# One start of a Fourier filter and ELU kernel, two ways of bringing in the filter

## The chip, the cores and the metric

The kernel runs on one core of a Trainium2 chip. A core has engines with in-order instruction streams of their own: TensorE (PE in the profile, its weight loads PEld), VectorE (DVE), ScalarE (ACT), GpSimd (POOL) and SyncE (SP). SP, ACT and POOL also issue DMA transfers, which all run on the same 16 DMA engines of the core; a transfer that SP issues stands in the queue q1 of the profile, one of ACT's in q10, one of POOL's in q0. Engines wait for one another, and for transfers, on semaphores.

The metric is the device time of one execution in microseconds (us). Before the change it was 2668.45 us, the median of three runs from 2663.02 to 2669.16.

## The reference

Two blocks follow each other. The first filters along the sequence in the frequency domain, the second is a two-layer network with ELU between:

```python
# x: (8, 3008, 256); filt_r, filt_i: (1505, 256)
X = np.fft.rfft(x, axis=1)
Y = X * (filt_r + 1j * filt_i)[None]
y = np.fft.irfft(Y, n=3008, axis=1).astype(np.float32)
# w_in: (256, 2048), w_out: (2048, 256), both float64
h = y.reshape(24064, 256) @ w_in
g = np.where(h > 0, h, np.exp(np.minimum(h, 0)) - 1)
out = (g @ w_out).astype(np.float32)
```

## The kernel before

**The transform.** 3008 is 47 x 64, and the Fourier transform of a batch is done as two small ones by matmul. Step a goes over the 64: six chunks of x, each of up to 2 x 4 values of the 47 (rows i and 47 - i, for the real symmetry), meet a table (ta, tf). Step b goes over the 47 for eight groups g of four frequencies (b_unit): two matmul results, re and im, are multiplied on VectorE by the filter's two parts (L321 to L324). Step bi (bi_unit) goes back over the 47, its result is written to DRAM (y_write, yd) and read back in another order (y_read), and n_unit goes back over the 64. Between a and b there is a turn of the data as well: through DRAM (z) for batches 1 to 7, but by PE transposes (t_first) for batch 0.

**The network.** Each of the six n_units of a batch gives 256 (or 224) columns in each of two halves. Both products use seven multiplications of blocks in place of eight; the sums of weight blocks are made once, in w_join, and the sums of data in combine (L395 to L398) and in the tails of up_steps and down_steps. From the first n_unit on, a list of items (b, m, q) is walked, and the transform of the next batch is placed in between by a plan of quads (`at(quad, place, fn, ...)`). The order within each engine is thus the program's order.

**The start.** Before the first n_unit three things must happen at once. Batch 0 must go through the transform. The weights, 16 groups of 512 KB of float64 (w_fetch, k = 0 to 15), must be brought in and turned into float32 by integer and float operations: w_split on VectorE (L588, L589), w_float on ScalarE (L594 to L599), w_join on VectorE (L605 to L625). Group k is w_in or w_out of quarter q = k // 4. And the filter must lie in the layout of step b: partitions 0 to 47 and 64 to 111, with a row of the spectrum and the mirrored row beside each other.

For batch 0 the filter is read straight from filt_r and filt_i into one large tile ff of all eight groups, by f_read_first: 11 transfers each, filt_r on SP's queue and filt_i on POOL's, with rows of 2 KB and 1 KB. For batches 1 to 7 the filter is first rearranged from DRAM to DRAM into fd (f_arrange, placed at quad 3), and each group is then read from fd by two transfers with rows of 4 KB (f_read) into one of three buffers (fbufs).

The queues in the start: SP has the first half of each x chunk (L236), the table tf (L238), the small tables gr, gi, gf, eye, then filt_r, gb, tn. POOL has the second half of each x chunk (L237), all weight groups and filt_i. A fetch of a weight group waits for its buffer: groups 6 to 11 take the buffers of x chunks 0 to 5 and wait for TensorE's matmuls on them. TICKS says which weight group is turned into float32 at which group g of the b loop; split k and tick(k) (float of k, join of k - 1) stand around the work of group g.

**The end.** The last o_unit transposes on VectorE (L540) and issues 16 stores of 32 KB; for the very last one they go around the queues of SP, ACT and POOL.

The lines that the prediction's steps name are these: L237 x half 1, L300 filter pieces, L321 first product, L341 and L342 evacuations of bi_unit, L350 y_write, L359 y_read, L396 the first combination behind both evacuations of n_unit, L540 and L550 the last transposes and stores, L789 in the profile for the memsets of fbufs.

Of the kernel before, what the change touches and what calls it, by code (L numbers as in the profile page):

```python
# [28 lines left out]
B = 8  # L29
# [12 lines left out]
def _make_tables():  # L42

    n2, k2 = np.arange(N2), np.arange(K2)
    ta, tn = np.zeros((P, H, P)), np.zeros((P, H, P))
    for i in range(H):
        for h in range(2):
            if h and i == 0:
                continue  # L60
            n1 = N1 - i if h else i
            th = 2 * np.pi * (((N1 * n2[:, None] + n1) * k2[None]) % N) / N
            c, s = np.cos(th), -np.sin(th)
            c[:, 0], s[:, 0] = 1.0, 1.0 - 2.0 * (n2 % 2)
# [24 lines left out]
    gb[64:88, 1, 24:48], gb[88:112, 1, 0:24] = -s3, -s0  # L89

    m0, m3 = np.full((24, 1), 2 / N), np.full((24, 1), 2 / N)
    m0[0] = m3[23] = 1 / N
    s0[:, 0] = s3[:, 23] = 0.0
    gr[0:24, 1, 0:24], gr[24:48, 1, 24:48] = m0 * c0.T, m3 * c3.T
    gi[0:24, 1, 24:48], gi[24:48, 1, 0:24] = -m0 * s0.T, -m3 * s3.T
    lie = np.concatenate([2 * np.arange(24), 2 * np.arange(24) + 1])
    gb[:, :, lie] = gb[:, :, :48].copy()
    for t in (gr, gi):
        for o in (0, 64):
            t[o + lie] = t[o:o + 48].copy()  # L100
    gf = np.zeros_like(gb)
    for o in (0, 64):
        gf[o:o + 48] = gb[o:o + 48].reshape(2, H, 2, 64).swapaxes(0, 1).reshape(48, 2, 64)
    return [t.astype(np.float32) for t in (ta, tn, gb, gr, gi, tf, np.eye(P), gf)]


def order(m):
# [5 lines left out]
def kernel(  # L113
# [8 lines left out]
):  # L122
    nc = tc.nc

    ta_d, tn_d, gb_d, gr_d, gi_d, tf_d, eye_d, gf_d = [
        nc.inline_tensor(t, name=n + "_t").ap()
        for t, n in zip(_make_tables(), ("ta", "tn", "gb", "gr", "gi", "tf", "eye", "gf"))
    ]

    def pool(name, bufs, **kw):  # L130
# [17 lines left out]
    psO = pool("psO", 1, space=PSUM)  # L148
    psM = pool("psM", 1, space=PSUM)

    gb, gr, gi = (glob.tile([P, 2, 64], FP32, name=n) for n in ("gb", "gr", "gi"))

    w_in, w_out = ([glob.tile([P, 7, 2, P], FP32, name="%s%d" % (n, i)) for i in range(4)] for n in ("wi", "wo"))

# [63 lines left out]
    def x_place_first(c):  # L218
        if c < XBUFS:
            t = xp.tile([P, 2, 2, D], FP32, tag="xc", name="xc").rearrange("p k u d -> p (k u) d")  # L220
        else:
            t = t1p.tile([P, XC, D], FP32, tag="t1", name="x1")
        if c < 2:
            w = tnp.tile([P, 4, P], FP32, tag="tn", name="tn")
        else:
            if c % 2 == 0:
                tas["pair"] = t4p.tile([P, 4, D], FP32, tag="t4", name="t0").rearrange("p u (w f) -> p (u w) f", f=P)
            w = tas["pair"][:, 4 * (c % 2):4 * (c % 2) + 4, :]
        xs[0, c], tas[0, c] = t, w
        if c == 0:  # L230
            nc.vector.memset(t[HALVES[1], 0, :], 0.0)

    def x_load_first(c):
        t = xs[0, c]
        u = 1 if c == 0 else 0
        nc.sync.dma_start(t[HALVES[0]].rearrange("p u d -> p (u d)"), raw(x, XC * c, [[N1 * D, 64], [1, XC * D]]))  # L236
        nc.gpsimd.dma_start(t[HALVES[1], u:XC, :], raw(x, N1 - XC * c - u, [[N1 * D, 64], [-D, XC - u], [1, D]]))  # L237
        nc.sync.dma_start(tas[0, c], tf_d[:, 4 * c:4 * c + 4, :])  # L238

    def a_first(c):  # L240
        xt, w = xs.pop((0, c)), tas.pop((0, c))
# [39 lines left out]
            k = p * K2 + 4 * g  # L281
            nc.sync.dma_start(t[r:r + 24].rearrange("i u d -> i (u d)"), zs[b][:, k:k + 4, :].rearrange("i u d -> i (u d)"))

    def f_read(b, g):
        t = fbufs[(b * NG + g) % FBUFS]
        for a, r in enumerate((LO, HI)):
            nc.gpsimd.dma_start(t[r].rearrange("p c u d -> p (c u d)"), fd[g, a].rearrange("q c u d -> q (c u d)"))

    def f_read_first(t, c):


        src, queue = ((filt_r, nc.sync), (filt_i, nc.gpsimd))[c]
        for a in ((0, 1), (1, 0))[c]:
            r = a * 64
            queue.dma_start(t[r:r + 48:2, :, c, :, :].rearrange("q g u d -> q g (u d)"),
                            raw(src, 2 * a, [[64 * D, 24], [4 * D, NG], [1, 2 * D]]))
            for u in range(2):
                g0 = 1 if a == u == 0 else 0
                for j, n in ((0, 16), (16, 7)):
                    queue.dma_start(t[r + 1 + 2 * j:r + 2 * (j + n):2, g0:NG, c, u, :],  # L300
                                    raw(src, 64 * (j + 1) - 4 * g0 - 2 * a - u,
                                        [[64 * D, n], [-4 * D, NG - g0], [1, D]]))
            if a == 0:
                queue.dma_start(t[1:48:2, 0, c, 0, :], raw(src, 32, [[64 * D, 24], [1, D]]))

    def tile_mm(ps, table, k, rhs, special):
        for u, w, v in ((0, 1, 1), (1, 1, 0)) if special else ((0, 2, 0),):
# [227 lines left out]
    def o_unit(b, m):  # L535
# [5 lines left out]
                                in_=c.rearrange("p e (j k s) -> p j k e s", k=2, s=32)[:, 0:n, k])  # L541

        o = o.rearrange("p (u f k) e s -> p u f k (e s)", u=4, f=2)
        queues = itertools.cycle((nc.sync, nc.scalar, nc.gpsimd) if (b, m) == (B - 1, 5) else (nc.sync,))
        for k in range(2):
            for u, w, i in ((0, 3, 1), (3, 1, 0)) if m == 0 else ((0, 4, 4 * m),):
                for f in range(1 if i == 0 else 2):
# [7 lines left out]

    wds = {}

    def w_fetch(k):
        q, j = divmod(k, 4)

        if k in (3, 4):
# [11 lines left out]
            srcs = [moe_w_out.bitcast(U32)[ts(4 * q + 2 * (j - 2) + i, P), :] for i in range(2)]  # L573
        for i, s in enumerate(srcs):
            n = 512 // len(srcs)
            nc.gpsimd.dma_start(wd[:, ts(i, n), :].rearrange("p a w -> p (a w)"), s)

# [49 lines left out]
    def f_arrange():  # L627

        for c, src in enumerate((filt_r, filt_i)):
            for a in range(2):  # L630
                nc.gpsimd.dma_start(fd[:, a, 0:48:2, c, :, :].rearrange("g q u d -> q g (u d)"),
                                    raw(src, 2 * a, [[64 * D, 24], [4 * D, NG], [1, 2 * D]]))
                for u in range(2):
                    g0 = 1 if a == u == 0 else 0
                    nc.gpsimd.dma_start(fd[g0:NG, a, 1:47:2, c, u, :].rearrange("g q d -> q g d"),
                                        raw(src, 64 - 4 * g0 - 2 * a - u,
                                            [[64 * D, 23], [-4 * D, NG - g0], [1, D]]))

                g0 = 0 if a else 1
                nc.gpsimd.dma_start(fd[g0:NG, a, 47, c, :, :].rearrange("g u d -> g (u d)"),  # L640
# [4 lines left out]
    with tc.manual_schedule():  # L645


        TICKS = {0: 7, 1: 8, 2: 9, 3: 10, 4: 11, 5: 12, 7: 13, 8: 14, 9: 15}
        with tc.tile_pool(name="boot", bufs=1) as bp:
            ff = bp.tile([P, NG, 2, 2, D], FP32, name="ff")  # L650
            eye = bp.tile([P, P], FP32, name="eye")
            gf = bp.tile([P, 2, 64], FP32, name="gf")
            pq = [bp.tile([P, 2, D], FP32, name="pq%d" % i) for i in range(2)]
            zt[0] += [bp.tile([P, 16 * ROWS], FP32, name="zt%d" % i) for i in range(2)]

            for z in zt[0] + zt[1]:
                nc.gpsimd.memset(z.rearrange("p (k r) -> p k r", r=ROWS)[:, :, 48:64], 0.0)
            for c in range(NXC):
                x_place_first(c)
            for c in range(NXC):  # L660
                x_load_first(c)
                if c < 5:
                    w_fetch(c)
            nc.scalar.memzero(ff[:, 0:NG // 2])
            nc.vector.memset(ff[:, NG // 2:NG], 0.0)
            wtmp.append([kp.tile([P, 512], U32, tag=t, name=n) for t, n in (("k0", "wm"), ("k1", "we"))] +
# [3 lines left out]
                        [t1p.tile([P, XC, D], FP32, tag="t1", name="wfl").rearrange("p (a b) d -> p a (b d)", a=2)])  # L670
            for i, v in enumerate((1151.0 * 2 ** 23, 255.0 * 2 ** 23)):
                nc.vector.memset(edges[:, i:i + 1], v)
            for t, d in ((gr, gr_d), (gi, gi_d), (gf, gf_d), (eye, eye_d)):
                nc.sync.dma_start(t, d)
            f_read_first(ff, 0)

            def tick(k):
                w_float(k)
# [2 lines left out]
            for c in range(NXC):  # L681
# [2 lines left out]
                a_first(c)  # L684
                if c > 0:
                    w_join(c - 1)
                    w_fetch(c + 4)
                if c == 2:
                    f_read_first(ff, 1)
            for k in range(NXC + 4, 14):  # L690
                w_fetch(k)
            for g in range(4):
                t_first(g)
            w_split(NXC)
            tick(NXC)
            w_fetch(14)
            nc.sync.dma_start(gb, gb_d)
            tn_read(0, 0)
            for g in range(NG + 2):
                k = TICKS.get(g)  # L700
# [11 lines left out]
                    y_read(0, 0, (nc.sync, nc.scalar))  # L712
                if k:
                    tick(k)
                if g == 0:
                    w_fetch(15)
        w_join(15)
        for c in range(2):
            x_load(1, c)
# [13 lines left out]

        for c in range(2, XBUFS):
            at(c - 2, 0, x_load, 1, c)
        at(3, 1, f_arrange)
        for f in fbufs:
            at(4, 1, nc.vector.memset, f, 0.0)
        for b in range(B):
# [82 lines left out]
```

## Time and profile before

| | us |
|---|---|
| median of three runs | 2668.45 |
| profiled execution, own time | 2667.55 |
| its span | 2665.7 |
| PE busy | 2598.2 (97%) |
| DVE busy | 1843.5 (69%) |
| ACT busy | 1507.6 (57%) |
| POOL busy | 250.5 (9%) |

All times within the profile count from the begin of the span. Busy times of PE are those of pipelined matmuls with modelled ends. The share of the DMA engines is a mean over 16. "Issue" as a cause of idle time means that the profile shows nothing that the engine waited for. A group of instructions is named by the line that issues it, the engine, the operation, and the tiles, written ones first.

### The profile page before, as it was taken

Reading aid. Unit: us, or ns where it says so; the run is one execution under the profiler, and the core shown is the slowest. Engines: PE = TensorE matmul, PEld = TensorE weight load, DVE = VectorE, ACT = ScalarE, POOL = GpSimd, SP = SyncE. Lnnn points to the kernel's source line nnn. Section 1 sums busy time; section 2 is a strip of 40 time slices with the busy share of each in tenths; the row PEclk is TensorE's granted clock in tenths of the full one; section 3 lists DMA queues with packets and bytes.
Section 4 is the critical chain, followed back from the end, with each engine's and each line's share of the span. In section 5 each row is a group of like instructions: output and inputs, shape, how many; then the busy total and the mean of one; then the engine's idle time right before and its main releaser. Section 6 shows DMA issues by size and latency. Waiting matters only on the chain.

```text
span 2665.7 us, 37329 instructions
## 1 busy us (share of the span) xinstructions
PE 2598.2 (97%) x13508; PEld 2211.9 (83%) x13508; DVE 1843.5 (69%) x3203; ACT 1507.6 (57%) x2622; POOL 250.5 (9%) x305
## 2 busy tenths in 40 slices
PE   4799999999999999999999999999999999999998
PEld 3488789888898878988889878898789887898887
DVE  4876767677676776667766676676767677666665
ACT  5655555555555555555555555555555555555554
POOL 3031200012000120002100021001210011000000
PEclk7799999999999999999999999999999999999999
DMA  9454311443124221333314232133321233110010
GB/s 244 114 132 113 100 44 38 102 104 86 38 58 123 76 81 40 95 86 83 77 39 102 73 101 71 38 87 101 99 55 38 75 82 85 39 40 19 22 27 16
DMA packets 229272, 202.87 MB, mean 76 GB/s; under 512 B 132312, under 2 KB 195467, under 8 KB 229089
## 3 DMA queue, kind: packets, MB, share of 16 engines
q1 hardware_dynamic: 210449, 163.00, 24.6%
q0 software_dynamic: 17616, 36.87, 5.5%
q8 instruction: 107, 1.75, 0.3%
q10 hardware_dynamic: 1024, 0.62, 0.1%
q14 instruction: 76, 0.62, 0.1%
HBM read 128.45 MB, written 74.97 MB: 76 GB/s over the span
## 4 chain that ended last, share of the span: by engine, by line
PE 95%; DMA 2%; DVE 2%; ACT 0%; issue 0%; POOL 0%; POOLq 0%; SPq 0%; DVEq 0%; ACTq 0%
PE po L502 43%; PE phs L420 25%; PE phd L420 12%; PE pha L420 6%; PE psn L372 3%; PE pva L309 2%; PE psr L309 2%; PE psa L207 2%; DMA wd<-in_moe_w_out_dram 0%; DMA ff<-in_filt_i_dram 0%; DMA f<-in_moe_w_in_dram 0%; DMA wd<-in_moe_w_in_dram 0%; DMA f<-in_moe_w_out_dram 0%; PE pvb L309 0%; PE psi L309 0%
## 5 line engine op out<-in xcount | busy, mean ns | idle before, releaser
L502 PE MATMUL po<-g,wo 128*128 128x256 f32 (+1 forms) x5376 | 1296.7, 375 | 0.0
L502 PEld LDWEIGHTS po<-g,wo 128*128 128x128 f32 x5376 | 1015.0, 190 | 129.5 <-issue 16.2
L431 ACT ACTIVATE g<-phs 128x512 f32<-128x512 f32 (+1 forms) x576 | 338.7, 588 | 843.8 <-PE phs L420 843.1
L428 DVE TENSOR_TENSOR g<-phd,g 128x512 f32<-128x512 f32 (+1 forms) x384 | 259.6, 676 | 463.9 <-ACT e L438 278.1
L438 ACT ACTIVATE e<-e 128x512 f32<-128x512 f32 (+1 forms) x768 | 477.3, 621 | 24.3
L420 PE MATMUL phs<-y,wi 128*128 128x256 f32 (+1 forms) x1536 | 395.4, 380 | 0.0
L420 PE MATMUL phs<-ys,wi 128*128 128x256 f32 (+1 forms) x1536 | 387.7, 375 | 1.5 <-ACT g L431 1.5
L442 DVE SCALAR_TENSOR_TENSOR g<-e,g 128x512 f32<-128x512 f32 (+1 forms) x576 | 387.1, 672 | 0.2 <-ACT e L438 0.2
L437 ACT ACTIVATE e<-g 128x512 f32<-128x512 f32 (+1 forms) x576 | 352.8, 613 | 35.3 <-DVE g L428 29.2
L420 PEld LDWEIGHTS phs<-y,wi 128*128 128x128 f32 x1536 | 285.1, 190 | 83.2 <-ACT t L341 34.1
L420 PEld LDWEIGHTS phs<-ys,wi 128*128 128x128 f32 x1536 | 291.4, 190 | 35.4 <-ACT g L431 2.5
L442 DVE SCALAR_TENSOR_TENSOR g<-e,phs 128x512 f32<-128x512 f32 (+1 forms) x192 | 129.9, 676 | 139.1 <-ACT e L438 139.1
L420 PE MATMUL phd<-ys,wi 128*128 128x256 f32 (+1 forms) x768 | 193.9, 375 | 1.8 <-DVE g L428 1.8
L420 PE MATMUL phd<-y,wi 128*128 128x256 f32 (+1 forms) x768 | 193.7, 375 | 0.0
L420 PE MATMUL pha<-y,wi 128*128 128x256 f32 (+1 forms) x768 | 193.7, 375 | 0.0
L437 ACT ACTIVATE e<-phs 128x512 f32<-128x512 f32 (+1 forms) x192 | 112.9, 588 | 141.9 <-PE phs L420 141.0
L330 POOL TENSOR_TENSOR sr<-sr,sp 128x512 f32<-128x512 f32 x56 | 71.2, 1271 | 1243.3 <-DVE sp L323 1243.3
L420 PEld LDWEIGHTS phd<-ys,wi 128*128 128x128 f32 x768 | 145.7, 190 | 18.9 <-DVE g L428 2.5
L420 PEld LDWEIGHTS pha<-y,wi 128*128 128x128 f32 x768 | 145.9, 190 | 16.6
L420 PEld LDWEIGHTS phd<-y,wi 128*128 128x128 f32 x768 | 145.8, 190 | 16.5
L479 DVE TENSOR_TENSOR g<-g,g 128x512 f32<-128x512 f32 (+1 forms) x192 | 130.8, 681 | 6.7
L482 DVE TENSOR_TENSOR g<-g,g 128x512 f32<-128x512 f32 (+1 forms) x192 | 130.6, 680 | 6.6
(143 smaller groups left out, 2403.4 us busy)
## 6 DMA issues: line engine op xcount, KB each, us to landing
yd<-t SPq DMA_DIRECT2D x127, 192.0 KB
t<-yd SPq DMA_DIRECT2D x190, 128.0 KB
z<-t SPq DMA_DIRECT2D x84, 256.0 KB
f<-fd POOLq DMA_DIRECT2D x112, 192.0 KB, 3.6
t<-z SPq DMA_DIRECT2D x224, 96.0 KB
out_dram<-o SPq DMA_DIRECT2D x630, 32.0 KB
tn<-tn_t SPq DMA_DIRECT2D x48, 256.0 KB
xc<-in_x_dram SPq DMA_DIRECT2D x84, 128.0 KB
```

Source lines behind the costliest of these rows:

```text
L309: nc.tensor.matmul(ps[:, u:u + w, :], table[k, v, :], r[k, u:u + w, :], start=n == 0, stop=n == len(rhs) - 1)
L330: nc.gpsimd.tensor_tensor(out=sr, in0=sr, in1=p, op=ALU.add)
L372: nc.tensor.matmul(ps[:, ts(q, P)], t[:, i - 4 * m, ds(dh * P, P)], w[:, i - 4 * m, :], start=True, stop=True)
L420: nc.tensor.matmul(ps[:, a, 0:h], w_in[q][:, COMBO[n], a, :], y[n], start=start and a == 0, stop=True, skip_group_check=True)
L428: nc.vector.tensor_tensor(out=g[o], in0=i0, in1=i1, op=ALU.add)
L431: nc.scalar.activation(out=g[o], in_=i0, func=AXT.Copy)
L437: nc.scalar.activation(out=e, in_=src, func=AXT.Relu, scale=-1.0)
L438: nc.scalar.activation(out=e, in_=e, func=AXT.Exp, scale=-1.0)
L442: nc.vector.scalar_tensor_tensor(out=g[n], in0=es[n], scalar=1.0, in1=src, op0=ALU.subtract, op1=ALU.max)
L479: nc.vector.tensor_tensor(out=b12, in0=b22, in1=b12, op=ALU.subtract)
L482: nc.vector.tensor_tensor(out=g["t4"], in0=g["b21"], in1=g["t2"], op=ALU.subtract)
L502: nc.tensor.matmul(po[i][:, u, 0:h], w_out[q][:, COMBO[n], a, :], g[n][:, a, :], start=q == 0 and a == 0 and n in (1, 3, 6, 4), stop=True, ...
```

## The change

The filter is rearranged by f_arrange first of all, on POOL's queue ahead of every other transfer, and batch 0 reads its groups from fd by f_read into the eight parts of ff. f_read_first is gone. In f_arrange the pieces of 23 rows are split in 16 and 7, so that it has 28 transfers in place of 20. Weight groups 0 to 7, both halves of x and all tables go by SP's queue; POOL has, behind the rearrangement, groups 8 and 9, and then groups 10 to 13 in between the reads of the filter. The tables gb, gr, gi are one transfer (gs), eye and gf another (once), and the table tf comes in double chunks from chunk 2 on. Weight groups 6 and 7 are split and converted before the b loop rather than in it, and TICKS shifts: three of the groups now come after the last product. The 16 last stores go by SP and ACT.

```diff
@@ x_load_first(c)
-        nc.gpsimd.dma_start(t[HALVES[1], u:XC, :], raw(x, N1 - XC * c - u, [[N1 * D, 64], [-D, XC - u], [1, D]]))
-        nc.sync.dma_start(tas[0, c], tf_d[:, 4 * c:4 * c + 4, :])
+        nc.sync.dma_start(t[HALVES[1], u:XC, :], raw(x, N1 - XC * c - u, [[N1 * D, 64], [-D, XC - u], [1, D]]))
+        if c < 2:
+            nc.sync.dma_start(tas[0, c], tf_d[:, 4 * c:4 * c + 4, :])
+        elif c % 2 == 0:
+            nc.sync.dma_start(tas.pop(("pair", c // 2)), tf_d[:, 4 * c:4 * c + 8, :])
@@ f_read
-    def f_read(b, g):
-        t = fbufs[(b * NG + g) % FBUFS]
+    def f_read(b, g, t=None):
+        t = fbufs[(b * NG + g) % FBUFS] if t is None else t
@@ f_read_first is removed
@@ o_unit
-        queues = itertools.cycle((nc.sync, nc.scalar, nc.gpsimd) if (b, m) == (B - 1, 5) else (nc.sync,))
+        queues = itertools.cycle((nc.sync, nc.scalar) if (b, m) == (B - 1, 5) else (nc.sync,))
@@ w_fetch
-    def w_fetch(k):
+    def w_fetch(k, queue=nc.gpsimd):
-            nc.gpsimd.dma_start(wd[:, ts(i, n), :].rearrange("p a w -> p (a w)"), s)
+            queue.dma_start(wd[:, ts(i, n), :].rearrange("p a w -> p (a w)"), s)
@@ f_arrange
-                    nc.gpsimd.dma_start(fd[g0:NG, a, 1:47:2, c, u, :].rearrange("g q d -> q g d"),
-                                        raw(src, 64 - 4 * g0 - 2 * a - u,
-                                            [[64 * D, 23], [-4 * D, NG - g0], [1, D]]))
+                    for j, n in ((0, 16), (16, 7)):
+                        nc.gpsimd.dma_start(fd[g0:NG, a, 1 + 2 * j:2 * (j + n):2, c, u, :].rearrange("g q d -> q g d"),
+                                            raw(src, 64 * (j + 1) - 4 * g0 - 2 * a - u,
+                                                [[64 * D, n], [-4 * D, NG - g0], [1, D]]))
@@ the start
-        TICKS = {0: 7, 1: 8, 2: 9, 3: 10, 4: 11, 5: 12, 7: 13, 8: 14, 9: 15}
+        TICKS = {0: 8, 1: 9, 3: 10, 5: 11, 7: 12, 8: 13, 9: 14}
+            f_arrange()
+            w_fetch(0, nc.sync)
             for c in range(NXC):
                 x_place_first(c)
             for c in range(NXC):
                 x_load_first(c)
-                if c < 5:
-                    w_fetch(c)
+                if 0 < c < 5:
+                    w_fetch(c, nc.sync)
-            for t, d in ((gr, gr_d), (gi, gi_d), (gf, gf_d), (eye, eye_d)):
-                nc.sync.dma_start(t, d)
-            f_read_first(ff, 0)
+            nc.sync.dma_start(once, once_d)
             for c in range(NXC):
                 w_split(c)
                 w_float(c)
                 a_first(c)
                 if c > 0:
                     w_join(c - 1)
-                    w_fetch(c + 4)
-                if c == 2:
-                    f_read_first(ff, 1)
-            for k in range(NXC + 4, 14):
-                w_fetch(k)
+                    w_fetch(c + 4, nc.sync if c < 4 else nc.gpsimd)
+            nc.sync.dma_start(gs, gs_d)
+            for g in range(NG):
+                f_read(0, g, ff[:, g])
+                if g % 2:
+                    w_fetch(NXC + 4 + g // 2)
             for g in range(4):
                 t_first(g)
-            w_split(NXC)
-            tick(NXC)
-            w_fetch(14)
-            nc.sync.dma_start(gb, gb_d)
+            for k in (NXC, NXC + 1):
+                w_split(k)
+                tick(k)
+                w_fetch(k + 8)
             tn_read(0, 0)
             for g in range(NG + 2):
...
                 if k:
                     tick(k)
-                if g == 0:
-                    w_fetch(15)
+            w_split(15)
+            tick(15)
         w_join(15)
@@ the plan
-        at(3, 1, f_arrange)
```

More of the change, by code (lines that the diff above doesn't have):

```diff
@@ L103, in _make_tables @@
         gf[o:o + 48] = gb[o:o + 48].reshape(2, H, 2, 64).swapaxes(0, 1).reshape(48, 2, 64)
-    return [t.astype(np.float32) for t in (ta, tn, gb, gr, gi, tf, np.eye(P), gf)]
+    once = np.stack([np.eye(P), gf.reshape(P, P)], 1)
+    return [t.astype(np.float32) for t in (ta, tn, np.stack([gb, gr, gi], 1), tf, once)]
 def order(m):
@@ L123 @@
     nc = tc.nc
-    ta_d, tn_d, gb_d, gr_d, gi_d, tf_d, eye_d, gf_d = [
+    ta_d, tn_d, gs_d, tf_d, once_d = [
         nc.inline_tensor(t, name=n + "_t").ap()
-        for t, n in zip(_make_tables(), ("ta", "tn", "gb", "gr", "gi", "tf", "eye", "gf"))
+        for t, n in zip(_make_tables(), ("ta", "tn", "gs", "tf", "once"))
     ]
@@ L149 @@
     psM = pool("psM", 1, space=PSUM)
-    gb, gr, gi = (glob.tile([P, 2, 64], FP32, name=n) for n in ("gb", "gr", "gi"))
+    gs = glob.tile([P, 3, 2, 64], FP32, name="gs")
+    gb, gr, gi = (gs[:, i] for i in range(3))
     w_in, w_out = ([glob.tile([P, 7, 2, P], FP32, name="%s%d" % (n, i)) for i in range(4)] for n in ("wi", "wo"))
@@ L226, in x_place_first @@
             if c % 2 == 0:
-                tas["pair"] = t4p.tile([P, 4, D], FP32, tag="t4", name="t0").rearrange("p u (w f) -> p (u w) f", f=P)
-            w = tas["pair"][:, 4 * (c % 2):4 * (c % 2) + 4, :]
+                tas["pair", c // 2] = t4p.tile([P, 4, D], FP32, tag="t4", name="t0").rearrange("p u (w f) -> p (u w) f", f=P)
+            w = tas["pair", c // 2][:, 4 * (c % 2):4 * (c % 2) + 4, :]
         xs[0, c], tas[0, c] = t, w
@@ L282, in z_read @@
             nc.sync.dma_start(t[r:r + 24].rearrange("i u d -> i (u d)"), zs[b][:, k:k + 4, :].rearrange("i u d -> i (u d)"))
-    def f_read(b, g):
-        t = fbufs[(b * NG + g) % FBUFS]
+    def f_read(b, g, t=None):
+        t = fbufs[(b * NG + g) % FBUFS] if t is None else t
         for a, r in enumerate((LO, HI)):
             nc.gpsimd.dma_start(t[r].rearrange("p c u d -> p (c u d)"), fd[g, a].rearrange("q c u d -> q (c u d)"))
[L289 to L304, printed above, removed]
     def tile_mm(ps, table, k, rhs, special):
@@ L645 @@
     with tc.manual_schedule():
-        TICKS = {0: 7, 1: 8, 2: 9, 3: 10, 4: 11, 5: 12, 7: 13, 8: 14, 9: 15}
+        TICKS = {0: 8, 1: 9, 3: 10, 5: 11, 7: 12, 8: 13, 9: 14}
         with tc.tile_pool(name="boot", bufs=1) as bp:
             ff = bp.tile([P, NG, 2, 2, D], FP32, name="ff")
-            eye = bp.tile([P, P], FP32, name="eye")
-            gf = bp.tile([P, 2, 64], FP32, name="gf")
+            once = bp.tile([P, 2, P], FP32, name="once")
+            eye, gf = once[:, 0], once[:, 1].rearrange("p (v q) -> p v q", v=2)
             pq = [bp.tile([P, 2, D], FP32, name="pq%d" % i) for i in range(2)]
```

## The prediction

> **What bounds the kernel now.** I read the page's forty slices first, then stretches of ten microseconds over the start, then the waits and the order of time there, and last the end. From slice 3 TensorE is full: a change at the ends of the kernel is worth what it moves the begin of that full stretch, or cuts from the last stores.
>
> ```profile
> PE   4799999999999999999999999999999999999998
> DMA  9454311443124221333314232133321233110010
> ```
>
> The stretches show who is idle while. Columns: stretch, its length, busy time of PE, PEld, DVE, ACT, POOL, clock, DMA share, GB/s.
>
> ```profile
> 30.00:40.00 10.00, 4.74 (x32) 4.58 (x31) 8.63 (x19) 6.84 (x17) 4.85 (x8) 0.83 1.08 209
> 40.00:50.00 10.00, 4.37 (x42) 2.90 (x40) 0.00 (x0) 4.71 (x9) 3.80 (x7) 0.80 1.01 207
> 50.00:60.00 10.00, 0.00 (x0) 0.00 (x0) 0.76 (x2) 2.53 (x4) 1.65 (x3) 0.50 1.04 278
> 60.00:70.00 10.00, 6.21 (x26) 3.29 (x26) 7.60 (x15) 3.40 (x6) 1.08 (x2) 0.50 0.46 160
> 70.00:80.00 10.00, 8.50 (x47) 3.52 (x45) 9.83 (x21) 7.42 (x14) 0.52 (x1) 0.84 0.26 64
> ```
>
> Two regimes: up to 62 us the DMA engines are full (share 1.0) and VectorE starves, from 38.9 to 62.4 almost wholly; from there to 119 VectorE is full (9.8 of 10) and DMA is not. VectorE's waits in the first 125 us, and what ends the long one:
>
> ```profile
> DVE wm L588 <- DMA wd<-in_moe_w_out_dram: 12.0, 2, 11.6
> DVE sr L321 <- issue: 11.1, 1, 11.1
> DVE we L605 <- ACT we L599: 2.8, 1, 2.8
> ...
> 36.27 11.17 SPq L300 DMA_DIRECT2D ff<-in_filt_r_dram  x4
> 47.48 0.44 SPq L697 DMA_DIRECT2D gb<-gb_t  x1
> 62.37 0.69 DVE L321 TENSOR_TENSOR sr<-psr,ff 128x512 f32<-128x512 f32 x1 [11.10 <-issue]
> ```
>
> The first filter product starts at 62.37, though its PE inputs were ready near 42. The page calls that "issue", but the last pieces of filt_r were issued on SP only by 47.4, and the trace's landing records have the last of them at 62.1: the whole of ff is waited for. Call this start T0. From it VectorE works through eight products (b_unit, 2.43 us each) and weight groups 6 to 15, and the first combination of n_unit runs at 120.69 (L396); TensorE is full from there.
>
> **What the Trainium skill says.** "DMA: Bandwidth & Descriptors", section "Queues, rings and completion order": each DMA engine takes turns between the queues, a packet at a time. The trace agrees: beside each other, POOL's queue (q0) and SP's (q1) get equal numbers of packets, and bytes by packet size. First 5 to 25 us, then 25 to 30, where q1 carried the 512-byte rows of the small tables:
>
> ```profile
> q0 software_dynamic: 1034, 3.52, 60.3%
> q1 hardware_dynamic: 1038, 2.45, 42.9%
> ...
> q0 software_dynamic: 369, 1.28, 85.8%
> q1 hardware_dynamic: 367, 0.24, 19.0%
> ```
>
> (Packets, MB, share.) Same page, "Issuing engines are not separate DMA queues": moving a transfer to another queue adds no bandwidth; here 298 GB/s in 5 to 25 us is the sum of both. Same page, "Two DMAs through the same engine are not ordered": who reads what a DMA wrote must wait for that DMA to complete; so every read of fd waits for the rearrangement, and the program does wait.
>
> **The change part by part.**
>
> *Rearranged first.* The 20 DMAs at quad 3 become 28 (23 rows split in 16 and 7) at the head of POOL's queue. Removed are 22 direct filter reads, 3.1 MB, half of them on SP; added are 3.15 MB from DRAM to DRAM and 16 reads of 192 KB (3.15 MB). So before the products are through, 3.15 MB more must pass. Issue: 28 x 0.6 us (the 16- and 7-row forms take 0.56 to 0.78 on POOL) = 17 us from 1.75. At q0's 3.52 MB in 20 us = 176 GB/s, it lands by about 24 us. Nothing of POOL's passes before it; x half 1 (L237) and weights 0 to 7 move to SP.
>
> *x, tables, weights by SP.* SP must now bring, in order, everything up to weight group 5: 5 groups besides it, x and tables, 7744 KB = 7.93 MB. x half 1 has 1 KB rows and half of the weights 2 KB rows there, against 4 KB packets on q0, so in each such stretch SP gets a fifth to a third. Behind the rearrangement POOL has w8 and w9, which wait for TensorE's chunks 2 and 3, the reads of ff 0 and 1 (together 1.84 MB), then w10, which waits for chunk 4, and ff 2 and 3 (1.31 MB). Bytes through before w5 is there: 3.15 + 7.93 + 1.84 = 12.9 MB, or 14.2 with the second group. At 298 GB/s, from 2.5 us, with 1.5 us to land: 47.3 or 51.7 us. I take 51, since w10 and its two reads have the larger packets just when x5's 1 KB rows pass. In the kernel before, w5's conversion on ScalarE began at 31.11.
>
> *From w5 to T0.* The trace gives this stretch: ScalarE at 31.11 takes w5, evacuates chunk 5 (to 35.4), then eight evacuations of t_first (0.7 us of the way spent on the late eye, to 42.3), then the conversion of w6 (to 44.7): 13.6 less 0.7. Now the join of w6 (2.0) and the split of w8 (0.7) stand before the first product on VectorE: T0 = 51 + 15.6 = 66.6. ff 0, issued at about 34, has landed; the filter is off the path, and the weights and x have taken its place.
>
> *From T0 on.* To the end of the eighth product: 8 x 2.43 + joins 7 to 10 (3.8 + 2.05 + 3.8 + 2.0) + four splits of 0.68 = 33.9 us (41.0 before; two groups fewer lie in it). After it the order is worse than before. ScalarE needs the split of w13 behind the 3.8 us join of w11, so the last evacuation (L341) ends at +7.9 (+5.4 before). ScalarE then issues y_read and waits there for y_write to land (3.2 us, as at 108.86 to 111.86, behind which the 2.8 us wait of VectorE above arose); now conversions 14 and 15 both are queued behind it: 7.9 + 0.4 + 3.2 + 0.5 + 2 x 2.6 = +17.2, the join of w15 3.75, one combination 0.4: L396 at +21.3 (+17.3 before). n_unit's matmuls, +12 + 3.8 + 3.75 = +19.5, are just hidden. Sum: T0 + 55.2 = 121.8, against 120.7: +1.1 us.
>
> *Middle.* f_arrange at 161 to 199 goes. In 160 to 185 TensorE is busy 25 of 25 us; it loses 1.82 us at 189.61 to VectorE, behind three memsets of 0.91 (L789), which stay. Cost nothing, hidden under TensorE; at most 1.8 us are to be had.
>
> *End.* 16 last stores go by SP and ACT, 8 each, in place of 6, 5 and 5.
>
> ```profile
> L817 SPq EVENT_SEMAPHORE  x12: 17/28/87, 2660.1 to 2665.6; - x12
> L817 POOLq EVENT_SEMAPHORE  x4: 17/17/17, 2664.9 to 2665.6; - x4
> L817 POOLq DRAIN  x3: 46/106/5732, 2659.2 to 2665.4; - x3
> L817 SPq DRAIN  x3: 7/7/7, 2662.1 to 2665.2; - x3
> ```
>
> SP has seen all landings at 2662.1, but POOL's drain of 5.7 us, behind its stores, goes on to 2664.9. Then 0.8 us to the end. With SP's 0.47 us per store (2.80/6), 8 end at 2660.7, landing seen 2.3 later = 2663.0, + 0.8 = 2663.8: -1.9 us. If POOL's drain is paid after SP's whatever is issued (2.8 more), it is +0.9. I take -1.9: POOL's queue will then have been still for hundreds of us.
>
> *Small edits.* Five tables become two (same bytes, three issues of 0.3 us fewer), four tf reads two: hidden under the full DMA engines. If SP's issue were the limit, they would give 1.5 us.
>
> Sum against the span of 2665.7: +1.1 + 0 - 1.9 = -0.8, 2664.9. The profiled execution's own time was 1.9 above its span, and the median 0.9 above that, so 2668.45 - 0.8 = 2667.6.
>
> **The rivals.** *A, the forecast:* DMA stays the bound of the start, the filter's place in it taken by w5. Break-even, the end counted in, is T0 = 67.4. *B, faster:* the two queues don't hinder each other: the rearrangement takes only lanes that SP leaves idle, and POOL's second group comes late. 12.9 MB at 320 GB/s put w5 at 44 us, T0 at 59.6: -5.9 - 1.9 = -7.8, 2660.6; at 350, which single slices of 1.75 us reach in the start (up to 364), w5 is there at 41: 2657.5. For it: VectorE's 23 idle us, and products that wait for one step of ff instead of all. Against it: packet counts. *C, slower:* copying from DRAM to DRAM has both sides in HBM and the filter's short rows, and holds the engines longer. When such copies ran, 160 to 200 us, both queues together moved 5.60 MB, 140 GB/s, though with 23-row forms that go now; while the filter was read at 30 to 45 us they moved 195 GB/s. If the first 22 us go at 140 in place of 298, 3.2 MB are left over, 10.5 us: T0 = 77, +11.6 - 1.9 = 2678. It decides (over +0.3%) from w5 at 59.8. *D:* the end gains nothing, or loses 0.9: 2670; it moves no sign by itself.
>
> **How the numbers follow.** A 0.56 (2661 to 2675), B 0.21 (2655 to 2661), C 0.18 (2674 to 2688), D with A's start 0.05. 0.3% is 8 us, about what a measurement of this kernel can tell from no change: below 2660.4 lies most of B and a little of A, 0.21; above 2676.5 most of C and a little of A, 0.19; within 0.60. Time 2667.6, range 2658 to 2679, which leaves a tenth out on each side.
>
> **What would show it.** Right, if the first split of w5 and its conversion start at 47 to 55 us, the reads of ff 0 have landed long before L321's first start, and that start is at 62 to 71; if q0 and q1 again have equal packet counts up to 25 us; if after the eighth product VectorE waits about 3 us for ScalarE's conversion behind y_read; and if POOL's drain ends before SP's. The forecast is wrong if w5 is there by 44 or after 60, if VectorE's first product waits for ff itself, or if TensorE loses more or less than 1.8 us at quad 4.

## The result, and the profile after

The changed kernel takes 2665.16 us (median of four executions, 2663.96 to 2667.51) against 2668.49 us of the kernel before (four executions): ratio 0.9993, 95% interval 0.9976 to 1.001. A second comparison on another occasion, 12 executions against 40, gave 2667.52 against 2667.43: 1.0001, 0.9992 to 1.0009. There is no difference that can be told, and the forecast was 2667.6. Executions of one and the same program spread over 7 us. Three programs have two profiled executions each: the spans of a pair differ by 1.4, 4.2 and 5.2 us, and the time up to the first combination by 1.3, 4.2 and 5.7, so the spread lies in the start.

The profiled executions have the same span, 2665.7 us, from parts that cancel. First the forty slices of the page after:

```profile
PE   4799999999999999999999999999999999999998
DMA  9533411343124231333314242133421233110010
```

TensorE's row is, digit for digit, that of before. The stretches over the start have the columns that were given with those of before (PE, PEld, DVE, ACT, POOL, clock, DMA share, GB/s):

```profile
30.00:40.00 10.00, 5.14 (x23) 4.58 (x22) 4.06 (x10) 4.90 (x11) 3.49 (x7) 0.50 1.06 290
40.00:50.00 10.00, 3.72 (x16) 3.49 (x16) 3.90 (x11) 3.18 (x8) 2.36 (x5) 0.50 1.04 253
50.00:60.00 10.00, 6.80 (x61) 5.17 (x60) 6.47 (x14) 9.51 (x20) 4.88 (x9) 0.96 1.05 276
60.00:70.00 10.00, 5.79 (x23) 3.09 (x24) 9.83 (x22) 5.85 (x11) 4.54 (x8) 0.55 1.03 254
70.00:80.00 10.00, 10.00 (x44) 3.59 (x43) 7.27 (x14) 5.46 (x12) 0.00 (x0) 0.60 0.30 94
```

The DMA engines are full up to 70 us in place of 60. The hole in VectorE's work, 40 to 60 us before, is spread over 10 to 60 (2.16 and 4.85 us of work in the two stretches ahead of those shown, where it had 4.60 and 7.89). And there is a new one at 70 to 80, where VectorE is busy 7.27 us of ten while TensorE is busy all ten at a granted clock of 0.60. VectorE's waits in the first 130 us say whom it waits for (total, times, longest):

```profile
DVE wm L576 <- DMA f<-in_moe_w_in_dram: 17.4, 2, 11.5
DVE sr L309 <- PE psi L297: 7.0, 5, 3.1
DVE wm L576 <- DMA wd<-in_moe_w_in_dram: 5.6, 1, 5.6
...
DVE we L593 <- ACT we L587: 2.6, 2, 2.3
```

L309 is the first product of each filter group (L321 before). It no longer waits for ff, but five times for TensorE's results (psi is the second of the two matmul results of a group); the long waits are now those of L576, the splits of weight groups. In order of time around the group that ended the DMA-bound part, w5 (the ends of lines in brackets are the idle time before, and what ended it):

```profile
49.11 0.43 DVE L576 TENSOR_SCALAR wm<-f 128x512 uint32<-128x512 uint32 x1 [5.96 <-DMA f<-in_moe_w_in_dram]
49.17 0.69 ACT L582 ACTIVATE wfl<-f 128x512 f32<-128x512 uint32 x1 [6.79 <-DMA f<-in_moe_w_in_dram]
...
53.26 4.01 ACT L270 ACTIVATE t<-po 112x512 f32<-112x512 f32 x8 [0.42 <-PE po L269]
...
62.83 0.68 DVE L309 TENSOR_TENSOR sr<-psr,ff 128x512 f32<-128x512 f32 x1
```

w5's conversion starts at 49.17 (31.11 before), T0 is 62.83 (62.37), the eighth product ends at 103.37 (103.41), and the first combination of n_unit runs at 123.82 (120.69): the start is 3.1 us longer in this execution. From the combination to the start of the last transposition (2658.80; 2656.25 before) it is 2534.98 us (2535.56). From there to the end it is 6.92 us where it was 9.44. The instructions of the end (shortest/median/longest in ns, then first and last start):

```profile
L806 POOLq DRAIN  x3: 51/106/5969, 2273.9 to 2665.4; - x3
L806 SPq DRAIN  x3: 7/7/7, 2664.9 to 2665.2; - x3
```

POOL's long drain of 5.97 us is still there, but it now starts at 2273.9, and SP ends last. +3.1 - 0.6 - 2.5 = 0.0.

### The profile page after: what moved, and what is told of

Its sections match the earlier page's. It is cut to its first block, busy times and chain, and to the rows that moved or that the text cites. A ratio compares the mean times of both kernels' runs of the same rounds, so it can differ in the third digit from the quotient of the medians.

```text
span 2665.7 us, 37335 instructions
## 1 busy us (share of the span) xinstructions
PE 2601.9 (98%) x13508; PEld 2213.2 (83%) x13508; DVE 1843.9 (69%) x3203; ACT 1507.8 (57%) x2622; POOL 235.6 (9%) x295
## 4 chain that ended last, share of the span: by engine, by line
PE 95%; DMA 2%; DVE 1%; issue 0%; ACT 0%; SPq 0%; DVEq 0%; ACTq 0%
PE po L490 43%; PE phs L408 25%; PE phd L408 12%; PE pha L408 6%; PE psn L360 3%; PE pva L297 2%; PE psr L297 2%; PE psa L209 2%; DMA f<-in_moe_w_in_dram 1%; DMA xc<-in_x_dram 1%; PE pvb L297 1%; DMA wd<-in_moe_w_out_dram 0%; PE psi L297 0%; PE po L269 0%; DMA t<-yd 0%
```

## The experiments

The anchors used throughout are the start of w5's conversion on ScalarE (w5), T0, the end of the eighth product (where VectorE's next instruction starts), the first combination of n_unit, and the stretch from the last transposition to the end. Each run lists its profiled execution; where it was timed against the kernel before, the ratio has its interval.

### The rearrangement back at quad 3

```diff
-            f_arrange()
             w_fetch(0, nc.sync)
...
-                f_read(0, g, ff[:, g])
+                f_plain(g, ff[:, g])     # rows of 4 KB as they lie in filt_r and filt_i
...
+        at(3, 1, f_arrange)
```

Batch 0 then takes the filter's rows in their own order: it reads as many bytes in as many transfers, but its mirrored rows, and so batch 0's share of the result, are left out. The same holds for the run with both cures below.

> The changed kernel, but the rearrangement goes back to quad 3, and batch 0 reads its filter as 4 KB rows straight from filt_r and filt_i, so that batch 0 is multiplied by rows in the wrong place (that part of the computation is left out); same number and size of reads, 3.15 MB less ahead of them. Theory (the start is bound by bytes through the DMA engines, the rearrangement is 3.15 MB of them): w5 converts some 10 us earlier than 49.1, about 39; the first product starts at 52 to 54 in place of 62.8, the first combination behind n_unit 9 to 10 us earlier than 123.8. Rival (SP's queue with its eight transfers in flight and 1 KB rows is the limit, whatever POOL does): w5 at 47 to 49, first product at 61 to 63.

```profile
41.01 0.69 ACT L587 ACTIVATE wfl<-f 128x512 f32<-128x512 uint32 x1 [6.70 <-DMA f<-in_moe_w_in_dram]
56.44 0.68 DVE L314 TENSOR_TENSOR sr<-psr,ff 128x512 f32<-128x512 f32 x1
```

w5 is 8.2 us earlier, T0 6.4, the combination (116.58) 7.2; one execution took 2660.27 us, where the median of before was 2667.54. The rearrangement's bytes in the start cost about 7 us of the path, somewhat less than expected. The rival, SP's queue as the limit by itself, falls.

### Groups 8 and 9 held back

```diff
-        elif k in (10, 11):
+        elif k in (8, 9):
             wd = t1p.tile(...)
-        elif k in (6, 7, 8, 9, 15):
+        elif k in (6, 7, 10, 11, 15):
             wd = xp.tile(...)
```

Groups 8 and 9 take other buffers, which come free later. POOL's issues stand in a line, so the reads of ff behind them are held back too.

> The changed kernel with four buffers swapped: weight groups 8 and 9 take the buffers of x chunks 4 and 5, groups 10 and 11 those of chunks 2 and 3, so that POOL's queue is empty from the end of the rearrangement until chunk 4 is done; all bytes are the same. Theory (packet turns: what POOL sends between 27 and 49 us delays x 4, x 5 and w5 on SP's queue by its bytes): w5 converts at 40 to 43 in place of 49.1, first product at 53 to 57 in place of 62.8, the first combination at 114 to 118, time 6 to 9 us less than the changed kernel. Rival (total bytes before the first product count, in whatever order): the first product stays within 2 us of 62.8, because ff 0 or w6 and w7 are then late, and the time stays.

The median is 2659.49 us (six executions) against 2667.54 of before: ratio 0.9969, 0.9957 to 0.998. w5 41.52, T0 55.12, combination 116.03. Not a byte is gone. What is different is what POOL's queue carries while SP still brings w5. The queue tables over the stretch before w5 (packets, MB, share of 16 engines), for the changed kernel from 2 to 50 us:

```profile
q1 hardware_dynamic: 4120, 8.29, 62.3%
q0 software_dynamic: 2392, 5.81, 41.6%
```

with groups 8 and 9 held back, from 2 to 40:

```profile
q1 hardware_dynamic: 4077, 8.19, 78.1%
q0 software_dynamic: 1600, 3.15, 24.6%
```

In each, SP has carried 8.2 to 8.3 MB about when w5 is there; POOL has carried 5.81 MB in one, and in the other the 3.15 MB of the rearrangement alone. That makes a table with the run above and the one that follows:

| until us | SP, MB | POOL, MB | GB/s in all | w5 |
|---|---|---|---|---|
| 32, both cures | 8.09 | 0 | 270 | 32.91 |
| 40, rearrangement at quad 3 | 8.16 | 2.29 | 275 | 41.01 |
| 40, groups 8 and 9 held back | 8.19 | 3.15 | 298 | 41.52 |
| 50, the changed kernel | 8.29 | 5.81 | 294 | 49.17 |

Against the first row, each MB on POOL's queue delays w5 by 3.5 (second row), 2.7 and 2.8 us: the DMA engines were full, so bytes that nobody needs yet push back those that are needed.

### Both cures of the start at once

The edits of the last two together.

> Both cures of the start at once: the rearrangement back at quad 3 (first batch reads the filter's own rows in steps), and groups 8 and 9 held back. Theory (bytes and turns ahead of w5 add up): w5's conversion at 31 to 36, T0 at 45 to 50, combination at 107 to 111, time 2651 to 2656. Rival (either cure removes the same wait, and behind it stands another): w5 at 39 to 41, T0 at 53 or later, combination at 114 to 117, time 2658 to 2661.

```profile
q1 hardware_dynamic: 4013, 8.09, 105.5%
```

Up to 32 us POOL's queue has carried nothing (the table of 2 to 32 us has one row). w5 32.91, T0 48.20, combination 108.54, and one execution took 2652.19 us where the median of before was 2666.44. The two add up: from 123.8 the one takes 7.2, the other 7.8, both 15.3.

### The rearrangement on SP's queue behind w5

Groups 8 and 9 held back, the two edits to come (TICKS, y_read), and:

```diff
-            f_arrange()
             w_fetch(0, nc.sync)
...
-                    w_fetch(c + 4, nc.sync if c < 4 else nc.gpsimd)
+                    w_fetch(c + 4, nc.sync if c < 2 else nc.gpsimd)
+                if c == 1:
+                    f_arrange()          # its 28 transfers issued by nc.sync
```

> Three edits as before, and the rearrangement issued on SyncE's queue behind w5, groups 6 and 7 on GpSimd's. It asks whether the rearrangement's bytes cost time at any place ahead of the products, or only ahead of w5. Theory (only what passes before w5 delays the chain, and ff 0 then has until w5 + 13.7): w5's conversion at 31 to 36, rearrangement landed by 40 to 46, T0 at 48 to 53, combination at 104 to 109, time 2648 to 2653. Rival (bytes cost the same wherever they pass, since ff 0 is now waited for): T0 at 54 or later, VectorE's first product waiting for ff, combination at 111 or later, time 2655 or more.

The median is 2658.99 us (five executions; before 2667.43), ratio 0.9965, 0.9952 to 0.9978. w5 came at 36.08, at the edge of what was expected. Up to 35 us SP had carried 8.12 MB and POOL 1.05, the groups 6 and 7: against the first row of the table that is 3.0 us for each MB again. But T0 came at 59.00 and the combination at 115.32:

```profile
DVE sr L309 <- DMA ff<-fd: 7.4, 1, 7.4
```

The first product waits for ff, as the rival had it. Its reason is another, though. The engines were not full while the rearrangement was under way:

```profile
40.00:50.00 10.00, 8.14 (x59) 6.68 (x59) 5.61 (x12) 8.53 (x17) 0.00 (x0) 0.83 0.62 195
```

DMA share 0.62, 195 GB/s. SP issues these 28 transfers one by one from 27.83 to 52.72, at 0.55 to 1.05 us each, 20.0 us in all, and the last lands at 54.0. The first read of ff is issued at 54.81. So it was the issuing that set the pace here, and not the bytes; no run tested this on its own. The theory of the turn (only what passes before w5 delays the chain) holds for w5; its time for ff left out the issue.

### x's half and the first weights behind the rearrangement on POOL

```diff
-        nc.sync.dma_start(t[HALVES[1], u:XC, :], raw(x, ...))
+        nc.gpsimd.dma_start(t[HALVES[1], u:XC, :], raw(x, ...))
...
-            w_fetch(0, nc.sync)       # and groups 1 to 7
+            w_fetch(0)                # by GpSimd
```

This undoes the part of the change that moves transfers to SP's queue. It was run once, and then timed.

> The rearrangement first, but x's second half and weight groups 0 to 7 behind it on GpSimd's queue, as they were in the kernel before. Theory (a queue is a line: what stands behind the 28 issues waits for them and for their landing slots): x's half and group 0 are issued from 26 us on, the first matmuls near 32 to 35, w5's conversion at 52 to 60, T0 at 66 to 75, combination 8 to 15 us later than the 123.8 of the changed kernel, time 2672 to 2682. Rival (the sum of bytes before w5 sets its time, the queue doesn't matter): w5 at 47 to 51, combination within 2 us of 123.8.

w5 50.23, T0 65.57, combination 125.29, 2668.84 us in that one execution. The rival was nearer. Timed, beside the changed kernel again:

> The changed kernel with x's second half and groups 0 to 7 behind the rearrangement on GpSimd's queue, timed. In its one execution w5 came at 50.2 and the combination at 125.3. Theory now (the sum of bytes before w5 sets its time, whichever queue brings them): within 2 us of the changed kernel's repeat. Rival (the line on GpSimd costs, and one slow first look hid less or more): over 4 us slower than the changed kernel's repeat.

> The changed kernel itself, unaltered, beside the others of this call, for what the start differs by between executions. Theory (the start follows the DMA rate of the execution): T0 58 to 67, w5 46 to 53, with GB/s of the first 40 us in step; from the combination on the same 2535.0 us and 6.9 us at the end; ratio to the kernel before 0.998 to 1.0.

This form took 2671.5 us (12 executions), ratio 1.0013 (1.0005 to 1.0022) to the kernel before; the changed kernel beside it 2667.52, ratio 1.0001 (0.9992 to 1.0009). So the move is worth about 4 us, half of what the first theory said at the least, but more than nothing; neither expectation was met in full. The stretches of its second profiled execution suggest where it goes:

```profile
10.00:20.00 10.00, 0.00 (x0) 0.00 (x0) 0.00 (x0) 0.00 (x0) 6.24 (x12) 1.00 1.04 320
20.00:30.00 10.00, 0.00 (x0) 0.00 (x0) 0.00 (x0) 0.00 (x0) 8.98 (x17) 1.00 0.70 181
```

No compute engine has anything to do until 30 us, since x's second half stands behind POOL's 28 issues; yet what waits there is caught up later, as it isn't the bound. What is lost for good would be 20 to 30 us, where the DMA engines themselves ran at 0.70 and 181 GB/s (345 in the changed kernel's repeat: 1.6 MB more). By 50 us 11.96 MB had passed, where in the changed kernel it was 14.10. That fits w5 at 51.45 and T0 at 66.81, against 47.75 and 62.45 in the repeat, but no run shows it alone.

### The weight groups one product apart

```diff
-        TICKS = {0: 8, 1: 9, 3: 10, 5: 11, 7: 12, 8: 13, 9: 14}
+        TICKS = {0: 8, 1: 9, 2: 10, 3: 11, 4: 12, 5: 13, 7: 14}
```

> The changed kernel with a weight group at each of the products 0 to 5 (groups 8 to 13), 14 at g = 7 and 15 last, as evenly as before. Theory (the 7.0 us that VectorE waits for PE's psi come from products 2, 4 and 6 having no weight group beside them to cover ScalarE's and TensorE's round): those waits fall under 2 us, the eighth product ends at about 103 as now or up to 2 us later, three groups in place of five lie after it, and the first combination comes 3 to 5 us earlier than 123.8; time 3 to 5 us less. Rival (the round over TensorE at half clock is the bound, VectorE's waits only show it): the eighth product ends 5 us later, the first combination stays within 1 us of 123.8.

The median is 2664.89 us (20 executions; before 2667.54), ratio 0.9989, 0.9982 to 0.9996. T0 62.96, the eighth product ends at 104.04, with two groups more in between than in the changed kernel, and the combination runs at 119.72, 4.1 earlier. VectorE's wait for psi went from 7.0 us to below one. That wait and the stretch 70 to 80 us, whose counterparts of the changed kernel stand above:

```profile
DVE sr L309 <- PE psi L297: 0.7, 2, 0.6
...
70.00:80.00 10.00, 10.00 (x42) 3.33 (x40) 9.86 (x18) 7.55 (x15) 0.00 (x0) 0.56 0.17 46
```

TensorE is as busy and its clock as low, but VectorE has 9.86 us of work beside it. The other runs bear it out: in all eight profiled executions with the TICKS of the change VectorE waits for psi 3.1 to 7.0 us, in all three with the even order 0.7 or 0.8. This is what was expected, but the repeat of the changed kernel adds a doubt about its size. There VectorE waited for psi 3.1 us, not 7.0, and the combination ran at 119.59 from nearly the same T0:

```profile
70.00:80.00 10.00, 10.00 (x58) 4.22 (x60) 8.51 (x15) 6.70 (x13) 0.00 (x0) 0.75 0.24 62
...
90.00:100.00 10.00, 9.87 (x74) 3.94 (x75) 8.89 (x17) 7.88 (x15) 0.00 (x0) 1.00 0.49 119
```

The clock that TensorE was granted was 0.75 and 1.00 in these stretches, 0.60 and 0.66 in the first execution. The Trainium skill, "TensorE: Matmul & The Clock Gate", section "Part 1: The HAM clock gate (the "warmup" mystery)", has the throttled state as the default, released by activity. The trace agrees only in part. In the changed kernel the clock was 0.50 at 30 to 50 us, where TensorE was busy 5.14 and 3.72 us of ten; but it was 0.60 at 70 to 80 us, where TensorE was busy all ten, and 0.80 at 40 to 50 us in the kernel before, with 4.37 us of work. What made two executions of one program differ isn't shown. The low clock and the long wait go together, though: from 90 to 100 us it was 1.00 in the two executions that waited 3.1 and 3.2 us, and 0.66 in the three others that started the products at about the same time and waited 5.9 to 7.0. From T0 to the combination it is 56.8 us with the even order, at the low clock, and 61.0 and 57.1 in the two executions of the changed kernel. So the order is worth 4.2 us at the low clock; at the high one the even order was not profiled. By time, ratios of 0.9989 here and of 0.9993 and 1.0001 for the changed kernel make it some 1 to 3 us, with intervals that overlap, so the time alone does not show a gain.

### y_read on SP alone

```diff
-                    y_read(0, 0, (nc.sync, nc.scalar))
+                    y_read(0, 0)
```

> The changed kernel with the four transfers of the first y_read all on SP's queue. Theory (ScalarE's queue holds conversions 14 and 15 behind its two issues, which wait for y_write): VectorE's 2.3 us wait before the join of w14 goes, joins end 2.3 to 2.6 us earlier, and the first combination comes at 121.5 to 122.5, then limited by n_unit, since four issues on one queue cost 0.7 us more. Rival (the wait is for the conversion's own inputs): the 2.3 us wait stays.

One execution took 2665.87 us. The combination runs at 122.16. From the end of the eighth product it is 19.08 us, where the changed kernel had 20.45 in both its profiled executions. In that stretch the wait for ScalarE's conversion (2.6 in the changed kernel's list above) is gone; a wait behind the next step has come:

```profile
DVE y L384 <- ACT y L362: 1.3, 1, 1.3
```

1.4 us gained of 2.6 taken away: the rest is about what this new wait takes, for n_unit's evacuation on ScalarE.

### The end alone

The kernel before, with only its last stores changed:

```diff
-        queues = itertools.cycle((nc.sync, nc.scalar, nc.gpsimd) if (b, m) == (B - 1, 5) else (nc.sync,))
+        queues = itertools.cycle((nc.sync, nc.scalar) if (b, m) == (B - 1, 5) else (nc.sync,))
```

> The kernel before, with only the last 16 stores dealt to SyncE and ScalarE instead of three queues. Theory (GpSimd's drain is paid after its last own instruction, out of sight when GpSimd isn't last): from the last transposition to the end of the span 6.9 to 7.0 us where it was 9.44, GpSimd's drain of some 5.7 to 6.0 us begins near 2270; the start as before (T0 62.4, combination 120.7), span end 2663 to 2663.4. Rival (the gain at the end came with the earlier changes of the program): 9.4 us again.

The end was 6.87 us, but the execution took 2669.24 us: its T0 was 66.32 and its combination at 125.53, though nothing there differs. In the first 2 to 22 us its DMA engines had moved 266 GB/s, in the profiled execution of before 295. It was then timed:

> The kernel before with the last 16 stores on SyncE and ScalarE alone, once more and timed, since in its first execution the end fell to 6.87 us as expected but the start was 4 us later at 270 in place of 300 GB/s. Theory (the start's DMA rate differs between executions; the end's gain of 2.5 us is real): over several runs 2 to 3 us under the kernel before, ratio 0.9985 to 0.9995; last transposition to end 6.9. Rival (the edit itself makes the start later): ratio 1.0005 to 1.0015.

The median is 2664.98 us over 20 executions, 2667.43 for before: ratio 0.9992, 0.9985 to 0.9998. The end took 6.86 us:

```profile
L817 POOLq DRAIN  x3: 46/98/6550, 2270.6 to 2662.1; - x3
L817 SPq DRAIN  x3: 7/7/7, 2661.5 to 2661.8; - x3
```

The whole gain of the change at the end, 2.5 us, is that of this one line. POOL's long drain starts beside its own last instructions, at 2270 us here, and is over long before the end.

### Three edits together

Groups 8 and 9 held back, even TICKS, y_read on SP:

> Groups 8 and 9 held back, the weight groups of TICKS one product apart, and y_read on SyncE alone, together. Theory (three separate costs: the start's DMA turns, VectorE's waits for the pseudo-real products of TensorE, ScalarE standing behind y_read): they add up. Holding back brought the first combination of n_unit to 116.0 us, even ticks were worth 4.1, SyncE's y_read 1.7: combination at 109 to 112, span end 2651 to 2654, ratio to the kernel before 0.994 to 0.9955. Rival (they hide behind one another, since VectorE or n_unit's matmuls are full there): combination at 114 to 116, no better than holding back alone, ratio 0.9965 to 0.9975.

The median is 2655.93 us (five executions), before 2666.44 (nine): ratio 0.9962, 0.9949 to 0.9976. w5 39.42, T0 54.47, combination 111.22, within what was expected, and the wait for psi at 0.8 us. By time the last two edits add 2.5 us to the 8.0 of holding back alone, not the 4.8 that the combinations differ by, and the ratio expected was missed; the intervals of the two runs (0.9957 to 0.998 for the other) don't tell them apart. It is the fastest kernel of these that computes the whole of the reference.

## Why the prediction was right, and where its steps were not

**The time: right; the sign: not told.** Forecast -0.8 us, in the middle of a range of 21. Timed, the change came to -3.3 us in one comparison and +0.1 in the other. Since the end alone gives -2.5, the start came to something between a gain of 0.8 us and a loss of 2.6; the forecast had +1.1.

**What takes the filter's place: right, by bytes.** Step "x, tables, weights by SP" summed 12.9 or 14.2 MB before w5 and took 51 us; 14.10 MB moved from 2 to 50 us and w5 was at 49.17 (47.75 in the repeat). The reads of ff 0 landed at 42.5 and 44.1, 19 us before T0. The table above shows the same sum in four forms of the kernel. Two terms under it were wrong. The first is equal packets per queue: from 5 to 25 us it was

```profile
q1 hardware_dynamic: 2012, 3.79, 63.6%
q0 software_dynamic: 1272, 2.68, 40.3%
```

so SP got 59% of the bytes, not a fifth to a third. Equal counts would have meant 47%, since POOL's packets were 2.1 KB on average and not the 4 KB of the forecast. The Trainium skill, "DMA: Bandwidth & Descriptors", section "Queues, rings and completion order", has the turns only between queues with work waiting, and POOL's queue had gaps (0.05 MB from 16 to 19 us). Where it had none the counts were nearly equal, from 20 to 25 us:

```profile
q0 software_dynamic: 443, 1.01, 54.7%
q1 hardware_dynamic: 488, 0.90, 50.6%
```

The second term is the time of the 28 issues: 24.7 us (1.74 to 26.46), not 17. The issues themselves took 16.7 us, as forecast. The rest was waiting, since from the ninth on POOL issued a piece only when the one eight before it had landed, 6.5 to 9.3 us after its own issue. So the rearrangement was in fd at 32.9, not at 24. Neither moved the sum: what POOL didn't carry early it carried late.

**w5 to T0: a little short.** Forecast 15.6, measured 13.66. ScalarE's eight evacuations ran through in 4.01 us; taking over the stretch of before, which had more than one wait in it, made it 1.9 too long.

**T0 to the eighth product: this step failed.** Forecast 33.9, measured 40.5 us and, in the repeat, 36.7. The sum of VectorE's work in it was right (40.5 less the 7.0 of waiting is 33.5). What was left out is TensorE. With the new TICKS products 2, 4 and 6 have no weight group beside them, VectorE is then faster than TensorE at its granted clock, and it waits for psi: 7.0 us in one execution, 3.1 in the other, below one with the groups spread evenly in the run above. The cover for TensorE's matmuls was the weight groups' work, and the change moved it; the prediction costed the move as two groups fewer and didn't ask what they had covered. T0 came 3.8 us earlier than forecast and this was 6.6 longer, so two errors hid one another in part: that the sum came out so close is partly luck.

**The eighth product to the combination: right.** Forecast 21.3, measured 20.45 in both executions, with ScalarE standing behind y_read as described (17.28 before).

**Middle: right.** TensorE is busy 18.18 us of 20 from 180 to 200, in both kernels: it loses its 1.82 us again, without f_arrange.

**End: right in the mechanism, -2.5 in place of -1.9.** The eighth store of ACT ends 4.5 us after the start of the last transposition, as forecast; the landing was seen 1.6 us later, not 2.3.

**The rivals.** B (queues don't hinder each other) falls: every MB on POOL's queue cost w5 some 3 us, though SP got more of the bytes beside the rearrangement than equal turns would have given it. C (copying from DRAM to DRAM is slow) falls: with it, 2 to 40 us went at 305 GB/s, at 318 in the repeat, against 271 in the kernel before. D falls by the run of the end alone.

## What to carry to other kernels

Where the DMA engines are full, sum the bytes of every queue up to the transfer that the compute engines need next: in the four forms of the table it came later by about 3 us for each MB that the other queue carried first, and holding back two transfers that were needed late was worth 6 to 8 us with not a byte fewer. Where the engines stood partly idle, as with x's second half behind POOL's issues, the sum of the bytes alone would give too early a time. Before moving small work between engines' larger steps, ask which wait it had covered. And where two executions of one program differ by as much as the edit is worth, compare stretches that begin after the difference, or time many executions.

## What had not been expected of the hardware

- GpSimd ends its part of the program with a drain that starts beside its last own instructions. It took 4.0 to 7.4 us in the fourteen profiled executions: 4.01 where GpSimd issued 144 transfers in the whole program, 5.97 or 5.98 with 168, 6.54 and 6.55 with 173, 7.44 with 186; in the kernel before, with 178 and the last of them just ahead, 5.73. Why it differs isn't shown. It costs nothing when it lies early: dropping five stores from GpSimd's queue brought the end forward by 2.5 us.
- The rate of the full DMA engines differs between executions of the same program: 295 GB/s in the profiled execution of before from 2 to 22 us, 266 and 278 in two with the same start. T0 was then 62.4, 66.3 and 61.7, so the rate is not all of it.
- Issuing DRAM-to-DRAM pieces cost 0.55 to 1.05 us each on SP, with the 16 DMA engines at 0.62 of their time from 40 to 50 us; on POOL it was 0.5 to 0.8 us each, and 8 us of waits for landings besides.
- The granted clock of TensorE in a stretch where it is busy all the time can differ between two executions of one program, 0.60 and 0.75 from 70 to 80 us.
